# Transposed input for tiles 4 to 15, LayerNorm's factor applied behind the projections

## The chip, the cores and the metric

The kernel runs on one core of a Trainium2 chip. The metric is the device time of one execution in microseconds (us), shown as the median of several runs; the inputs are in the chip's memory before it starts. Engines are called by the names of the profile: PE (TensorE, matrix products), PEld (its weight loads), DVE (VectorE), ACT (ScalarE), POOL (GpSimd) and SP (SyncE, which issues all DMAs here).

## The reference

A block of 2048 tokens with 640 features: LayerNorm, attention with 32 heads of 20 features in a window of 256 tokens, a residual sum, and then a gated MLP that mixes tokens. Only the first part bears on this change:

```python
def _layernorm(x, axis=-1, eps=1e-5):
    m = jnp.mean(x, axis=axis, keepdims=True)
    v = jnp.var(x, axis=axis, keepdims=True)
    return (x - m) / jnp.sqrt(v + eps)

def _A_ref(x, wqkv, wo):
    B, S, D = x.shape                       # 1, 2048, 640
    H = 32; Dh = D // H; W = 256
    qkv = (lambda x, *d: x.transpose(*d))((x @ wqkv).reshape(B, S, 3, H, Dh), 2, 0, 3, 1, 4)
    q, k, v = qkv[0], qkv[1], qkv[2]
    scores = jnp.einsum("bhqd,bhkd->bhqk", q, k) * (Dh ** -0.5)
    ...
x = A_x
h = x + _A_ref(_layernorm(x, axis=-1), A_wqkv, A_wo)
```

LayerNorm's factor 1/sqrt(v + eps) is one number per token, so it may be applied to x before the product with the weights, or to the rows or columns of the product.

## The kernel before

**Value stage.** The tokens are 16 tiles of 128. For a tile i, `load_x` brings 128 tokens x 640 features; `ln1` (through `layernorm`, lines 74 to 80) takes its statistics on DVE (L74 to L76), raises the variance to the power -1/2 on POOL (L77) and subtracts the mean and multiplies by the factor on DVE (L80). `turn1` makes five transposes of 128x128 on PE (L469) into two PSUM banks; ACT copies them to a rounded high part (L473) and DVE makes the low part, the difference (L474). High and low parts of four tiles together fill one of the four chunks `xn_hi[c]`, `xn_lo[c]`, features first. `vgemm` multiplies a tile with the value weights: two halves of 320 columns, five feature blocks, three products each (high-high L485, high-low L486, low-high L487), so 30 products a tile, and ACT writes each half to `v_sb` (L488). The value weights arrive in raw form in ten pieces and are split by `split_wv`: the high part on ACT (L560), the low part on DVE or POOL (L561). A first stretch of 14 products with `ident` (L567) fills the time until the data is there.

**Query and key stage.** `qk_item(m, c)` makes one item: 128 rows m of queries or keys for the 512 tokens of chunk c, 15 products with 512 columns (L525 to L527), in one of two PSUM tiles. `split_qk` cuts the sum into three bf16 parts: ACT copies the first (L539), DVE subtracts it (L541), ACT copies the second (L543), POOL subtracts it for the third (L544), and SP stores all three to `qk_d` (L547). The steps of an item's split are issued during the next item's first two feature blocks. There are 40 items: 24 run alone, 4 more as a lead-in, and 12 are woven into the maximum stage.

**Maximum stage.** `max_item` makes scores for 128 queries against up to 384 keys (L333) and DVE takes each row's maximum (L339, one pass and one short reading of the result). 64 of these run with the 12 last items between them, one feature block of an item behind each. Each `max_item` takes one of three PSUM banks in turn. After eight blocks of queries `max_rows` turns the maxima into rows (L345, L348, L349). `load_stack` (L299) brings the stored parts back into the stacked form that the scores need.

PE, DVE, ACT and SP run their instructions in the order in which the code issues them; only POOL's order is left to the scheduler. So an instruction that waits holds up all behind it on its engine. The order at the start is written by hand:

```python
ln1(1, lambda: [split_wv(k, d, nc.vector) for k in (2, 4)])
for i in range(NT):
    if i + 3 < NT:
        load_x(i + 3)
    if i == 0:
        vgemm(0)
        ln1(2, lambda: turn1(1))
    elif i + 2 < NT:
        ln1(i + 2)
    if i == 1:
        vgemm(1)
    if 0 < i and i + 1 < NT:
        turn1(i + 1)
```

Of the kernel before, what the change touches and what calls it, by code (L numbers as in the profile page):

```python
# [34 lines left out]
def block_kernel(ctx, tc, x, wqk, wv, wo, w_in, wsp, bsp, w_out, out):  # L35
# [15 lines left out]
    r_d = dram.tile([H, S], F32, name="r_d")  # L51
    h_d = dram.tile([NT, P, D], F32, name="h_d")
# [175 lines left out]
    with ExitStack() as ab:  # L228
# [220 lines left out]
        if True:  # L449
# [3 lines left out]
            def load_x(i):  # L453
                xts[i] = tmp.tile([P, D], F32, tag="ta", bufs=3, name=f"xt{i}")
# [3 lines left out]
            def ln1(i, between=None):  # L458
                xn = tmp.tile([P, D], F32, tag="tb", bufs=2, name=f"xn{i}")
                layernorm(xn, xts.pop(i), D, f"a{i}", between)  # L460
# [15 lines left out]
            def vgemm(i):  # L476
                c, o = divmod(i, 4)
                t0 = o * P
                for j in range(2):
                    ps = s1_tile() if j else pv_tile(f"v{i}_{j}")  # L480
                    n0 = j * HD
                    for k in range(KD):
# [6 lines left out]
                                         ps[:, :HD].rearrange("p (h c) -> p h c", c=DH), AF.Copy)  # L489
# [3 lines left out]
            def load_wqk(m):  # L493
                raws[m] = tmp.tile([P, KD, P], F32, tag="wraw", bufs=5, name=f"wqraw{m}")
# [10 lines left out]
            def load_wo(k):  # L505
                raws[k] = tmp.tile([P, D], F32, tag="wraw", bufs=5, name=f"woraw{k}")
# [10 lines left out]
            def store_wo(k):  # L517
                for a, t in enumerate(wqs.pop(k)):
                    nc.sync.dma_start(wo_d[k, a], t.bitcast(F32))

# [15 lines left out]
            def split_qk(m, c, ps):  # L536
                sg = tmp.tile([P, 3, 512], BF16, tag="ta", bufs=3, name=f"sg{m}_{c}")
                rest = tmp.tile([P, 512], F32, tag="tb", bufs=2, name=f"rest{m}_{c}")
                nc.scalar.activation(sg[:, 0, :], ps, AF.Copy)  # L539
                yield  # L540
                nc.vector.tensor_tensor(out=rest, in0=ps, in1=sg[:, 0, :], op=OP.subtract)  # L541
                yield
                nc.scalar.activation(sg[:, 1, :], rest, AF.Copy)  # L543
# [8 lines left out]
            wv_raw = [tmp.tile([P, D], F32, tag="wraw", bufs=5, name=f"wvraw{k}") for k in range(KD)]  # L552
            for j, c in enumerate(halves):
                for k in range(KD):
                    nc.sync.dma_start(wv_raw[k][:, c], wv[k * P:(k + 1) * P, c])
                load_x(j + 1)
# [11 lines left out]
            ln1(0)  # L568
# [755 lines left out]
```

## Time and profile before

| what | us |
|---|---|
| median of 3 runs (lowest, highest) | 1129.86 (1129.74, 1132.98) |
| the profiled execution, its own time | 1132.73 |
| its span, first to last instruction | 1130.9 |
| PE busy in the span | 1093.7 |
| DVE busy in the span | 732.2 |
| ACT busy in the span | 565.9 |
| POOL busy in the span | 296.6 |
| value stage: first product of tile 0 to first query product | 8.86 to 91.86 |
| first maximum's scores to the last woven item's last product | 188.8 to 241.94 |

The profile is of one execution. A row of its timeline gives the start in us from the span's start, the duration in us, engine, line, operation, output and inputs, shapes, and in brackets the idle time of the engine just before and what ended it. PE's records overlap: a product's duration is longer than the distance to the next start, and the distance is what it takes of PE. A row of its busy times by stretches gives the stretch, its length, the busy us of the engines with the number of instructions, the clock that PE was granted (1.00 is full), the busy share of the DMA engines and the GB/s moved.

### The profile page before, as it was taken

Reading aid. Unit: us, or ns where it says so; the run is one execution under the profiler, and the core shown is the slowest. Engines: PE = TensorE matmul, PEld = TensorE weight load, DVE = VectorE, ACT = ScalarE, POOL = GpSimd, SP = SyncE. Lnnn points to the kernel's source line nnn. Section 1 sums busy time; section 2 is a strip of 40 time slices with the busy share of each in tenths; the row PEclk is TensorE's granted clock in tenths of the full one; section 3 lists DMA queues with packets and bytes.
Section 4 is the critical chain, followed back from the end, with each engine's and each line's share of the span. In section 5 each row is a group of like instructions: output and inputs, shape, how many; then the busy total and the mean of one; then the engine's idle time right before and its main releaser. Section 6 shows DMA issues by size and latency. Waiting matters only on the chain.

```text
span 1130.9 us, 28689 instructions
## 1 busy us (share of the span) xinstructions
PE 1093.7 (97%) x11180; PEld 986.3 (87%) x11180; DVE 732.2 (65%) x2060; ACT 565.9 (50%) x1169; POOL 296.6 (26%) x429
## 2 busy tenths in 40 slices
PE   8999999999999999889899999999999899999998
PEld 7998887667887777689799999999999799999998
DVE  6541123789999998478877678645458974656442
ACT  3433443249998989635566567433247521222210
POOL 3314444446666666612200011000001000000000
PEclk9999999999999999999999999999999999999999
DMA  5621346555565555489754522233251564444321
GB/s 183 224 72 68 136 141 239 176 178 170 184 188 175 181 170 158 143 241 305 255 185 165 181 90 76 85 122 101 100 162 57 176 193 135 123 148 138 103 87 61
DMA packets 83320, 171.78 MB, mean 152 GB/s; under 512 B 10944, under 2 KB 45248, under 8 KB 79296
## 3 DMA queue, kind: packets, MB, share of 16 engines
q1 hardware_dynamic: 83184, 169.95, 46.9%
q8 instruction: 88, 1.44, 0.6%
q14 instruction: 48, 0.39, 0.1%
HBM read 112.04 MB, written 57.87 MB: 150 GB/s over the span
## 4 chain that ended last, share of the span: by engine, by line
PE 74%; DVE 7%; DMA 7%; ACT 7%; issue 3%; POOL 1%; SPq 1%; DVEq 0%; ACTq 0%; POOLq 0%
PE g L1064 22%; PE out_ps L1129 8%; PE pv L425 5%; ACT pt L400 4%; PE zb L956 4%; PE qk L525 4%; PE qk L526 4%; PE qk L527 4%; PE bank L329 3%; PE bank L397 3%; PE zx L904 2%; PE zv L904 2%; DMA m<-o_d 2%; DMA wraw<-w_in_in 2%; PE zy L904 1%
## 5 line engine op out<-in xcount | busy, mean ns | idle before, releaser
L400 ACT ACTIVATE pt<-bank 128x384 f32<-128x384 f32 (+1 forms) x452 | 180.7, 477 | 19.9 <-PE bank L397 15.2
L721 ACT ACTIVATE aw<-fx 128x512 fp32r<-128x512 f32 (+2 forms) x160 | 93.5, 594 | 167.3 <-PE g L1064 122.6
L1064 PE MATMUL g<-zl,aw 128*128 128x432 f32 x768 | 171.8, 359 | 0.8 <-ACT zl L721 0.6
L339 DVE CUSTOM_DVE_ANT_0 junk<-bank,strip 128x288 bf16<-128x288 f32 x392 | 156.4, 454 | 14.0 <-PE bank L329 13.0
L1064 PEld LDWEIGHTS g<-zl,aw 128*128 128x128 f32 x768 | 143.7, 188 | 7.6 <-ACT zl L721 0.9
L425 PE MATMUL pv<-pt,v_sb 128*32 128x192 f32 (+3 forms) x1984 | 130.6, 322 | 7.5 <-ACT ot L441 3.5
L1064 PE MATMUL g<-ze,aw 128*128 128x432 f32 x576 | 134.8, 362 | 0.8 <-ACT aw L721 0.4
L715 DVE TENSOR_TENSOR aw<-fx,aw 128x512 fp32r<-128x512 f32 (+2 forms) x160 | 102.6, 646 | 37.9 <-ACT aw L721 36.7
L1064 PEld LDWEIGHTS g<-ze,aw 128*128 128x128 f32 x576 | 107.7, 189 | 7.0 <-ACT aw L721 1.6
L404 POOL TENSOR_SCALAR_AFFINE_SELECT pt<-pt 128x512 f32<-128x512 f32 x128 | 82.3, 644 | 61.9 <-ACT pt L400 58.2
L397 PE MATMUL bank<-slot 123*32 123x288 bf16 (+6 forms) x1296 | 94.0, 275 | 3.1 <-issue 2.2
L1129 PE MATMUL out_ps<-wout,y_sp 128*128 128x320 f32 (+1 forms) x630 | 96.2, 309 | 0.4 <-ACT y_sp L136 0.4
L956 PE MATMUL zb<-win,aw 128*128 128x432 f32 x480 | 95.3, 359 | 0.0
L1129 PEld LDWEIGHTS out_ps<-wout,y_sp 128*128 128x128 f32 (+1 forms) x630 | 94.1, 188 | 1.2 <-ACT y_sp L136 0.7
L329 PE MATMUL bank<-slot 120*32 120x288 bf16 (+6 forms) x1280 | 92.8, 277 | 1.9 <-DVE mcol L339 1.5
L956 PEld LDWEIGHTS zb<-win,aw 128*128 128x128 f32 x480 | 89.9, 187 | 5.0 <-ACT row L721 0.3
L86 POOL TENSOR_TENSOR mvz<-mvz,half 128x1 f32<-128x1 f32 x16 | 10.1, 633 | 303.3 <-DVE mvz L85 303.3
L541 DVE TENSOR_TENSOR rest<-qk,sg 128x512 f32<-128x512 f32 x40 | 27.7, 692 | 84.2 <-ACT sg L539 84.2
L425 PEld LDWEIGHTS pv<-pt,v_sb 128*32 128x32 f32 x1984 | 60.4, 110 | 18.7 <-issue 9.2
L715 DVE TENSOR_TENSOR row<-g,row 128x432 f32<-128x432 f32 x80 | 48.2, 604 | 37.6 <-PE g L1064 36.8
L407 POOL TENSOR_SCALAR_AFFINE_SELECT pt<-pt 128x512 f32<-128x512 f32 x112 | 72.5, 648 | 0.0
L397 PEld LDWEIGHTS <-slot 123*32 123x32 bf16 x1728 | 59.4, 97 | 14.1 <-issue 5.3
(185 smaller groups left out, 2233.0 us busy)
## 6 DMA issues: line engine op xcount, KB each, us to landing
slot<-qk_d SPq DMA_DIRECT2D x144, 160.0 KB
fx<-wsp_in SPq DMA_DIRECT2D x32, 512.0 KB
qk_d<-sg SPq DMA_DIRECT2D x40, 384.0 KB
fx<-hn_d SPq DMA_DIRECT2D x32, 320.0 KB
o_d<-ot SPq DMA_DIRECT2D x64, 128.0 KB
xb<-qk_d SPq DMA_DIRECT2D x48, 160.0 KB
z_d<-row SPq DMA_DIRECT2D x16, 432.0 KB
g_d<-row SPq DMA_DIRECT2D x16, 432.0 KB
```

The lines of the kernel that those rows point to most:

```text
L329: nc.tensor.matmul(ps[32 * j:32 * j + 32, o:o + w], one(st, 120, 0, hh, q0, 32), k, start=True, stop=True, tile_position=(0, 32 * j))
L339: nc.vector.tensor_tensor_reduce(out=junk[:, :n], in0=ps[:, :n], in1=keep, scale=1.0, scalar=NEG, op0=OP.add, op1=OP.max, accum_out=m_cols ...
L397: nc.tensor.matmul(ps[32 * i:32 * i + 32, b + o:b + o + w], one(st, 123, 1, hh, k0, 32), q, start=True, stop=True, tile_position=(0, 32 * i))
L400: nc.scalar.activation(pt[:, hh, :n], ps[:, :n], AF.Exp, scale=SCALE)
L404: nc.gpsimd.affine_select(out=pt[:, :, :P], in_=pt[:, :, :P], pattern=[[0, 4], [1, P]], base=0, channel_multiplier=-1, compare_op=OP.is_ge ...
L407: nc.gpsimd.affine_select(out=pt[:, :, 256:], in_=pt[:, :, 256:], pattern=[[0, 4], [-1, P]], base=-1, channel_multiplier=1, compare_op=OP. ...
L425: nc.tensor.matmul(ps[32 * hh:32 * hh + 32, a - 512 * c:b - 512 * c], v_sb[:, kb, v0:v0 + 32], pt[:, hh, a - kb * P:b - kb * P], start=fir ...
L715: (eng or nc.vector).tensor_tensor(out=out, in0=a, in1=b, op=op)
L721: nc.scalar.activation(out, a, AF.Copy)
L956: nc.tensor.matmul(b[0][:, :HF], a[t][:, x, kk], win2[0][:, y, kk, h * HF:(h + 1) * HF], start=kk + x + y == 0, stop=kk == KD - 1 and x == 1)
L1064: nc.tensor.matmul(ps, w[m][:, x, k], zc[k][m][:, y], start=start and k + x + y == 0, stop=stop and k == 3 and x == 1, skip_group_check=True)
L1129: nc.tensor.matmul(ps[j][:, :HD], src[:w, a, k, :], e1["wout"][:w, b, k, j * HD:(j + 1) * HD], start=(k == 0 and a + b == 0), stop=(k == K ...
```

## The change

The host lays x out a second time with the features first (`xt`). Tiles 0 to 3 keep their transposes on PE. For tiles 4 to 15 the transposed form is loaded (`load_xt`), and since the mean of a token is then needed along a row, `mean_row` makes it with one f32 product a tile: the column of means, spread over 128 columns, times `ident`, gives the means in every row. `turn1` subtracts that on DVE and makes high and low part from SBUF.

LayerNorm's factor is no longer applied to x. `stats1` leaves it in a column of `inv_std`. For the values it becomes the scale of ACT's copy to `v_sb`. For queries and keys it has to be a row over tokens: `store_std` transposes `inv_std`, stores it to `rstd_d`, and `load_std` loads the row of a chunk into all partitions. `split_qk` now begins with a multiplication by that row on DVE, which frees the PSUM tile, and the three parts are cut from the result in SBUF. So that one row serves two items, the 24 items run in pairs of m for each chunk. Buffers change with it: `ta` from 3 to 2, `tb` from 2 to 3, `wraw` from 5 to 3.

```diff
+            def stats1(i):
+                src = xts[i]
...
+                for j in range(2):
+                    nc.vector.bn_stats(out=st[:, j, :], in_=src[:, halves[j]])
+                nc.vector.bn_aggr(out=mv[:, 0:2], in_=st)
+                nc.vector.tensor_scalar(out=mv[:, 2:3], in0=mv[:, 1:2], scalar1=EPS, scalar2=None, op0=OP.add)
+                nc.gpsimd.tensor_tensor(out=inv_std[:, i:i + 1], in0=mv[:, 2:3], in1=half, op=OP.pow)
+
+            def center1(i):
+                xn = tmp.tile([P, D], F32, tag="tb", bufs=3, name=f"xn{i}")
+                nc.vector.tensor_scalar(out=xn, in0=xts.pop(i), scalar1=mvs.pop(i)[:, 0:1], scalar2=None,
+                                        op0=OP.subtract)
                 xns[i] = xn
+
+            def mean_row(i):
+                del xts[i]
+                rows1[i] = s2_tile()[:, :P]
+                nc.tensor.matmul(rows1[i], mvs.pop(i)[:, 0:1].to_broadcast([P, P]), ident, start=True, stop=True)
...
             def turn1(i):
                 xn = xns.pop(i)
                 c, o = divmod(i, 4)
+                if i >= TURNED:
+                    hi, lo = (v[c][:, :, o * P:(o + 1) * P] for v in (xn_hi, xn_lo))
+                    nc.vector.tensor_tensor(out=xn, in0=xn, in1=rows1.pop(i)[:, None, :].to_broadcast([P, KD, P]),
+                                            op=OP.subtract)
+                    nc.scalar.activation(hi, xn, AF.Copy)
+                    nc.vector.tensor_tensor(out=lo, in0=xn, in1=hi.bitcast(F32), op=OP.subtract)
+                    return
...
                     nc.scalar.activation(v4[:, i, 16 * j:16 * j + 16, :DH],
-                                         ps[:, :HD].rearrange("p (h c) -> p h c", c=DH), AF.Copy)
+                                         ps[:, :HD].rearrange("p (h c) -> p h c", c=DH), AF.Copy,
+                                         scale=inv_std[:, i:i + 1])
...
             def split_qk(m, c, ps):
-                sg = tmp.tile([P, 3, 512], BF16, tag="ta", bufs=3, name=f"sg{m}_{c}")
-                rest = tmp.tile([P, 512], F32, tag="tb", bufs=2, name=f"rest{m}_{c}")
-                nc.scalar.activation(sg[:, 0, :], ps, AF.Copy)
+                sg = tmp.tile([P, 3, 512], BF16, tag="ta", bufs=2, name=f"sg{m}_{c}")
+                rest = tmp.tile([P, 512], F32, tag="tb", bufs=3, name=f"rest{m}_{c}")
+                nc.vector.tensor_tensor(out=rest, in0=ps, in1=stds[c], op=OP.mult)
                 yield
-                nc.vector.tensor_tensor(out=rest, in0=ps, in1=sg[:, 0, :], op=OP.subtract)
+                nc.scalar.activation(sg[:, 0, :], rest, AF.Copy)
                 yield
+                nc.vector.tensor_tensor(out=rest, in0=rest, in1=sg[:, 0, :], op=OP.subtract)
                 nc.scalar.activation(sg[:, 1, :], rest, AF.Copy)
...
-            ln1(1, lambda: [split_wv(k, d, nc.vector) for k in (2, 4)])
+            stats1(1)
+            center1(1)
+            load_x(3)
+            for k in (2, 4):
+                split_wv(k, d, nc.vector)
             for i in range(NT):
-                if i + 3 < NT:
-                    load_x(i + 3)
                 if i == 0:
                     vgemm(0)
-                    ln1(2, lambda: turn1(1))
-                elif i + 2 < NT:
-                    ln1(i + 2)
-                if i == 1:
-                    vgemm(1)
-                if 0 < i and i + 1 < NT:
-                    turn1(i + 1)
+                    turn1(1)
+                    for n in (2, 3):
+                        stats1(n)
+                        center1(n)
+                        if n == 2:
+                            load_x(4)
+                else:
+                    if i + 3 < NT:
+                        load_xt(i + 3)
+                    if i + 4 < NT:
+                        load_x(i + 4)
+                    if i + 1 < NT:
+                        turn1(i + 1)
+                if TURNED <= i + 3 < NT:
+                    stats1(i + 3)
+                if TURNED <= i + 2 < NT:
+                    mean_row(i + 2)
...
-                if i > 1:
+                if i:
                     vgemm(i)
```

How the rows stand on PE at the start, before (`bank` and `v` are PSUM tiles, `xn_195` is tile 1, `xn_243` tile 2, `xn_263` tile 3, `slot` the value weights):

```order
L487 MATMUL bank_117<-slot_0_98,xa 128x320
L469 MATMUL bank_118<-ident,xn_195 128x128 x4
L469 MATMUL bank_119<-ident,xn_195 128x128
L485 MATMUL v_0_272<-slot_0_98,xa 128x320
...
L487 MATMUL bank_116<-slot_0_98,xa 128x320
L469 MATMUL bank_120<-ident,xn_243 128x128 x4
L469 MATMUL bank_118<-ident,xn_243 128x128
L469 MATMUL bank_119<-ident,xn_263 128x128 x4
L469 MATMUL bank_120<-ident,xn_263 128x128
```

And now (`xn_204` is tile 1, `xn_261` tile 2, `xn_272` tile 3, `mva_288` the statistics of tile 4):

```order
L528 MATMUL bank_118<-slot_0_99,xa 128x320
L510 MATMUL bank_119<-ident,xn_204 128x128 x4
L510 MATMUL bank_120<-ident,xn_204 128x128
L510 MATMUL bank_121<-ident,xn_261 128x128 x4
L510 MATMUL bank_119<-ident,xn_261 128x128
L526 MATMUL v_0_296<-slot_0_99,xa 128x320
...
L528 MATMUL bank_117<-slot_0_99,xa 128x320
L510 MATMUL bank_120<-ident,xn_272 128x128 x4
L510 MATMUL bank_121<-ident,xn_272 128x128
L485 MATMUL bank_119<-ident,mva_288 128x128
```

Tile 2's transposes have moved ahead of tile 1's products, and a mean row stands where two tiles' transposes followed each other. On DVE the same place read, from the end of tile 1's statistics to tile 2's normalising pass:

```order
L76 TENSOR_SCALAR mva_197<-mva_197 128x1
L561 TENSOR_TENSOR slot_1_99<-wvraw_129,slot_0_98 128x320
L561 TENSOR_TENSOR slot_1_99<-wvraw_131,slot_0_98 128x320
L80 TENSOR_SCALAR xn_195<-xt_137,mva_197 128x640
L74 BN_STATS sta_244<-xt_144 128x6 x2
L75 BN_AGGR mva_245<-sta_244 128x2
L76 TENSOR_SCALAR mva_245<-mva_245 128x1
L474 TENSOR_TENSOR xa<-bank_118,xa 128x4x128
L474 TENSOR_TENSOR xa<-bank_119,xa 128x128
L80 TENSOR_SCALAR xn_243<-xt_144,mva_245 128x640
```

And now:

```order
L473 TENSOR_SCALAR mva_198<-mva_198 128x1
L478 TENSOR_SCALAR xn_204<-xt_139,mva_198 128x640
L612 TENSOR_TENSOR slot_1_100<-wvraw_131,slot_0_99 128x320
L612 TENSOR_TENSOR slot_1_100<-wvraw_133,slot_0_99 128x320
L515 TENSOR_TENSOR xa<-bank_119,xa 128x4x128
L515 TENSOR_TENSOR xa<-bank_120,xa 128x128
L471 BN_STATS sta_254<-xt_170 128x6 x2
L472 BN_AGGR mva_255<-sta_254 128x2
L473 TENSOR_SCALAR mva_255<-mva_255 128x1
L478 TENSOR_SCALAR xn_261<-xt_170,mva_255 128x640
```

Tile 1 is centred (L478) ahead of the last two splits of the value weights, and tile 2's statistics stand behind tile 1's low part (L515) instead of ahead of it. In the maximum stage, DVE had between two items of a cycle (`junk` and `mcol` are a maximum and its reading, `rest` is an item's remainder, `qk` its PSUM tile):

```order
L339 ISA junk_2_2_1867,mcol_0_1788<-bank_115,mask 128x384
L339 ISA mcol_0_1788 128x1
L541 TENSOR_TENSOR rest_1_1870<-qk_1_1833,sg_1_1869 128x512
L339 ISA junk_2_3_1878,mcol_0_1788<-bank_117,mask 128x384
L339 ISA mcol_0_1788 128x1
```

And now:

```order
L587 TENSOR_TENSOR rest_1_1915<-qk_1_1878,std_1_1684 128x512
L340 ISA junk_4_0_1923,mcol_0_1792<-bank_116,mask 128x384
L340 ISA mcol_0_1792 128x1
L591 TENSOR_TENSOR rest_1_1915<-rest_1_1915,sg_1_1914 128x512
L340 ISA junk_4_1_1933,mcol_0_1792<-bank_118,mask 128x384
```

The multiplication (L587) stands one maximum ahead of the subtraction (L591), which needs ACT's copy of the product in between.

More of the change, by code (lines that the diff above doesn't have):

```diff
@@ L551, in block_kernel @@
             load_x(0)
-            wv_raw = [tmp.tile([P, D], F32, tag="wraw", bufs=5, name=f"wvraw{k}") for k in range(KD)]
+            wv_raw = [tmp.tile([P, D], F32, tag=("wraw", "wqh")[k > 2], bufs=(3, 4)[k > 2], name=f"wvraw{k}")
+                      for k in range(KD)]
             for j, c in enumerate(halves):
```

80 lines of the change are left out of this document (57 added, 23 removed).

## The prediction

> **What bounds the kernel now.** First the page: its first row says that TensorE is never far from busy, so a gain has to be a matmul that goes or a gap that closes. Then the busy time by stretches, since the change touches only the first 250 us.
>
> ```profile
> PE 1093.7 (97%) x11180; PEld 986.3 (87%) x11180; DVE 732.2 (65%) x2060; ACT 565.9 (50%) x1169; POOL 296.6 (26%) x429
> 30.00:40.00 10.00, 10.00 (x72) 9.99 (x71) 5.56 (x16) 4.64 (x11) 4.19 (x4) 1.00 0.65 229
> 200.00:220.00 20.00, 19.62 (x92) 12.34 (x90) 15.21 (x49) 4.91 (x8) 9.55 (x9) 1.00 0.54 174
> 220.00:240.00 20.00, 20.00 (x98) 12.80 (x97) 15.62 (x52) 6.06 (x10) 6.46 (x5) 1.00 0.60 196
> ```
>
> The columns after the stretch are its length and the busy us of PE, PEld, DVE, ACT and POOL, then clock, DMA share and GB/s. In the value stage (about 7 to 92 us) and where queries and keys are projected, PE has no gap and VectorE has room. In the maximum stage (189 to 242 us) PE is also full, but VectorE is at 15.2 to 15.6 of 20 us, and the change adds to it just there.
>
> **Saved on PE.** The timeline of PE around one value tile gives the price of its five transposes:
>
> ```profile
> 27.94 0.31 PE L487 MATMUL bank<-slot,xa 128*128 128x320 f32 x1
> 28.09 0.71 PE L469 MATMUL bank<-ident,xn 128*128 128x128 f32 x5
> 28.55 0.39 PE L485 MATMUL v<-slot,xa 128*128 128x320 f32 x1
> 28.78 0.31 PE L486 MATMUL v<-slot,xa 128*128 128x320 f32 x1
> 91.86 0.39 PE L525 MATMUL qk<-xa,wqh 128*128 128x512 f32 x1
> ```
>
> From the start of the transposes to the next product are 0.46 us, and that product takes 0.23 us to the next one where the others take 0.147: 0.085 more. A tile pays 0.545 us; 12 tiles pay 6.5 us. The check: from the start of tile 2's products (23.60, below) to 91.86 are 68.26 us, and 14 x 30 x 0.1467 + 12 x 0.545 = 68.2.
>
> **Added on PE.** Twelve mean rows and one transpose. No row shows a mean row in its place: it is f32, not a transpose, so two records. Nearest by place is the transpose, of the same shape and type at 0.46 / 5 = 0.09 us each: two make 0.18, 0.22 with some of the lead-in. The other end is the warm-up product, which is of the same kind:
>
> ```profile
> 1.77 5.96 PE L567 MATMUL bank<-ident 128*128 128x128 f32 x28 [1.77 <-POOL ident L59]
> ```
>
> 28 records for 14 products, 0.43 us each; with the lead-in 0.51. I take 0.22, since the warm-up stands at the program's start and the transposes stand where the mean rows will. The Trainium skill, "TensorE: Matmul & The Clock Gate", section "What's actually happening", says that the array starts at half its clock until it has been busy for about 3.4 us; by that the 0.43 would be 0.21 in a warm stage, while the page shows 1.00 there and so can't confirm it. 12 x 0.22 = 2.6, and 0.1 for the one transpose: **net -3.8 us**, between -6.5 + 2.2 + 0.1 = -4.2 and -6.5 + 6.1 + 0.1 = -0.3.
>
> The VectorE and ScalarE work per value tile stays about as it was (a normalising pass of 612 ns and two subtractions go, a subtraction of the mean and one low part come), within 5.6 of 10 us. Transfers grow by 320 KB a tile on a DMA share of 0.65 with 229 GB/s; each load is issued two tiles ahead, about 9 us, so I cost them at nothing. If that cover went, a late tile would stop PE for the lateness.
>
> **Lost at the start.** Here the order on PE and VectorE changes, and PE waits.
>
> ```profile
> 13.46 0.89 DVE L561 TENSOR_TENSOR slot<-wvraw,slot 128x320 fp32r<-128x320 f32 x2
> 14.01 0.41 PE L486 MATMUL bank<-slot,xa 128*128 128x320 f32 x1 [0.50 <-DVE slot L561]
> 14.40 0.61 DVE L80 TENSOR_SCALAR xn<-xt,mva 128x640 f32<-128x640 f32 x1
> 15.29 0.71 PE L469 MATMUL bank<-ident,xn 128*128 128x128 f32 x5
> 16.55 0.89 DVE L474 TENSOR_TENSOR xa<-bank,xa 128x512 fp32r<-128x512 f32 x2 [0.31 <-ACT xa L473]
> 17.36 0.60 DVE L80 TENSOR_SCALAR xn<-xt,mva 128x640 f32<-128x640 f32 x1
> 17.88 0.88 DVE L74 BATCH_NORM_STATS2 sta<-xt 128x6 f32<-128x320 f32 x2
> 19.03 0.15 DVE L76 TENSOR_SCALAR mva<-mva 128x1 f32<-128x1 f32 x1
> 23.60 0.39 PE L485 MATMUL v<-slot,xa 128*128 128x320 f32 x1
> ```
>
> Tile 1 is now centred before the two last splits of the value weights, which PE waits for at 14.01: 0.54 us later (14.40 to the next start at 14.93 in the row's own place). Tile 1's transposes move from 15.29 to 15.83, its low part from 16.55 to 17.09, ending after 0.81 at 17.90. Only then come tile 2's statistics, 1.23 us to the centring, and the centring of 0.61: 19.74. Tile 2's transposes now stand ahead of tile 1's products on PE, so **PE stands from about 16.4 to 19.8**; before, it ran tile 1's products there. They start at 19.80 + 0.47 = 20.27, tile 3's transposes at 20.27 + 4.48 = 24.75, tile 2's products at 25.22 without the mean row. Before it was 23.60: **+1.6 us**. I bound it by 1.0 (centring costs nothing at 14.01) and 2.5 (tile 2's load, issued behind tile 0's centring, lands after 17.90).
>
> **The clock.** That gap of 3.3 us may cost again. The stretches of 3.41 us that go with the two drops in the trace, and one without:
>
> ```profile
> 243.02:246.43 3.41, 1.63 (x34) 0.78 (x37) 3.37 (x18) 1.26 (x4) 2.55 (x3) 0.96 0.09 32
> 246.43:249.84 3.41, 3.41 (x64) 2.66 (x67) 2.86 (x14) 3.41 (x9) 2.43 (x6) 0.54 0.66 190
> 560.46:563.87 3.41, 1.34 (x8) 0.94 (x6) 0.47 (x1) 1.07 (x3) 0.72 (x2) 1.00 0.95 340
> 894.97:898.38 3.41, 1.24 (x7) 0.86 (x7) 3.41 (x7) 2.09 (x5) 0.00 (x0) 0.96 0.62 208
> ```
>
> After 1.63 and 1.24 us busy the clock went to about half for 3.41 us; after 1.34 it did not. A gap of 3.3 us leaves one such stretch with under 1.3 us busy in about two of three placements, and half speed for 3.41 us costs up to 1.7. I take **+1.3**, between 0 and 1.7; and the existing slow stretch at 246 may fall away in another placement, -1.7. The same page of the Trainium skill, section "HAM oscillation — how this bites in real kernels", warns only of PE gaps above about 3.4 us; by that this gap costs nothing and the sum is 1.3 lower, but the row at 243.02 shows a drop after a stretch that was never wholly idle.
>
> **Lost in the maximum stage.** Each of the 40 query and key items gets one more VectorE pass, from PSUM, and keeps its subtraction. Where PE has only these items, VectorE is mostly idle and the accumulator is free after one pass instead of two, so nothing is lost. In the maximum stage VectorE's cycle of five maxima is this:
>
> ```profile
> 198.11 0.69 DVE L541 TENSOR_TENSOR rest<-qk,sg 128x512 f32<-128x512 f32 x1
> 198.72 0.55 DVE L339 CUSTOM_DVE_ANT_0 junk<-bank,mask 128x384 bf16<-128x384 f32 x1
> 199.29 0.56 DVE L339 CUSTOM_DVE_ANT_0 junk<-bank,mask 128x384 bf16<-128x384 f32 x1
> 200.16 0.56 DVE L339 CUSTOM_DVE_ANT_0 junk<-bank,mask 128x384 bf16<-128x384 f32 x1 [0.30 <-PE bank L333]
> 202.47 0.69 DVE L541 TENSOR_TENSOR rest<-qk,sg 128x512 f32<-128x512 f32 x1
> 197.41 0.60 ACT L539 ACTIVATE sg<-qk 128x512 bf16<-128x512 f32 x1 [2.16 <-PE qk L527]
> 244.76 0.24 PE L329 MATMUL bank<-slot 120*32 120x128 bf16 x4 [1.26 <-DVE mcol L339]
> ```
>
> A cycle is 4.37 us of PE. VectorE uses 0.61 (198.11 to 198.72) + 5 x 0.57 = 3.46. Now 0.61 comes for the scaling, and the subtraction waits for ScalarE, which can start when the scaling ends: scaling at 0, copy at 0.72, subtraction 0.70 later (197.41 to 198.11) at 1.42, while the maximum between them ends at 1.18: 0.24 of waiting. 3.46 + 0.61 + 0.24 = 4.31 of 4.37: PE still decides, with three banks of slack, but VectorE can't catch up. The row of maxima halfway adds some 0.6 that stays: I take 0.35 of lateness at the end. There PE already waits 1.26 us for VectorE (244.76), so the last item's 0.61 + 0.24 and that lateness go straight on the path: **+1.2**, between 0.6 and 3.
>
> **Sum.** -3.8 + 1.6 + 1.3 + 1.2 = +0.3 us on the profiled execution's 1132.73 (span 1130.9 and 1.8 around it), so 1133.0 there. That execution lies 2.9 above the median of 1129.86, whose runs reach from 1129.74 to 1132.98; on the median the sum gives **1130.2**. A measurement of this kernel tells about 0.3%, 3.4 us, from no change.
>
> **Rivals.** *The gaps cost little*: the clock holds and the tail takes 0.6: -3.8 + 1.6 + 0.6 = -1.6, 1128.3, and with the slow stretch at 246 gone 1126.6; a mean row of 0.18 and a start of 1.0 bring 1125.5. For it speaks the row at 560.46, against it the row at 243.02.
>
> *VectorE becomes the bound of the maximum stage* (slower). It decides when its cycle passes 4.37, which 0.06 us is enough for. The subtraction now reads only SBUF, as the splits of the value weights do:
>
> ```profile
> 5.70 0.48 DVE L561 TENSOR_TENSOR slot<-wvraw,slot 128x320 fp32r<-128x320 f32 x1
> 11.14 1.17 DVE L561 TENSOR_TENSOR slot<-wvraw,slot 128x320 fp32r<-128x320 f32 x1
> ```
>
> The same pass took 0.48 alone and 1.17 beside GpSimd's. Were each subtraction 0.5 longer, 12 cycles would lose 12 x (4.81 - 4.37) = 5.3, less one bank's slack of 0.9: 0.3 + 4.4 gives 1134.6. The two output buffers instead of three could do the same through a late copy. Against it: GpSimd's pass of the item before ends about 0.4 us before the scaling starts. The Trainium skill, "SBUF — State Buffer", section "SBUF: two separate sides", says that VectorE with two SBUF inputs and GpSimd reading SBUF exclude each other for a whole instruction; the two rows agree, and by it the loss hangs on that 0.4 us.
>
> *The change does not save PE time*: a mean row at 0.51 costs 12 x 0.29 = 3.5 more: 1133.7.
>
> **How the numbers follow.** Forecast 0.67, gaps cheap 0.17, VectorE-bound 0.11, mean row dear 0.05. Of the second a half, and a little of the first, is faster than 1126.5: faster 0.10. Slower than 1133.2 are the third, most of the fourth and a few hundredths of the first: 0.15. Same: 0.75. The range leaves out the far ends of the second and third: 1126.4 to 1133.9; the forecast's own is 1127.5 to 1132.
>
> **What would show it.** The first query item should start near 89.7 + 1.3 instead of 91.86; a gap of some 3.3 us on PE, ended by VectorE's centring, should stand near 16.5; a clock row of about 0.5 soon behind it; the mean rows should be two records within 0.2 us; VectorE at 18 of 20 us in the maximum stage with PE full; the wait at its end about 2.4 instead of 1.26. I am wrong if PE waits inside the maximum stage, if loads stop PE between 25 and 60 us, or if the gap at 16.5 is filled.

## The result, and the profile after

| | before | after |
|---|---|---|
| median of 19 runs each on one chip, us (the lowest) | 1132.51 (1128.9) | 1139.38 (1134.63) |
| ratio of after to before, 95% interval | | 1.0053 [1.0037, 1.007] |
| the profiled execution's own time | 1132.73 | 1139.72 |
| its span | 1130.9 | 1138.0 |

The change makes the kernel slower by half a per cent; on the 1129.86 of the prediction the ratio gives 1135.8, above the range. One of after's 19 runs took 2159.28 us, and the ratio leaves it out. The two profiles differ by 7.1 us of span and the medians by 6.9; a second profile of before (e15) is 1.9 us longer than the first, so the totals of two profiles alone prove little. The page's first row and the busy time by stretches, of the kernel after:

```profile
PE 1096.5 (96%) x11145; PEld 986.1 (87%) x11145; DVE 759.2 (67%) x2088; ACT 569.2 (50%) x1158; POOL 297.1 (26%) x429
```

```profile
30.00:40.00 10.00, 10.00 (x71) 10.00 (x70) 5.61 (x13) 4.63 (x8) 4.32 (x5) 1.00 0.70 221
200.00:220.00 20.00, 19.86 (x91) 12.46 (x89) 17.03 (x55) 5.65 (x9) 9.27 (x7) 1.00 0.53 176
220.00:240.00 20.00, 19.97 (x99) 12.77 (x99) 17.30 (x54) 5.72 (x10) 7.11 (x7) 1.00 0.63 205
17.74:21.15 3.41, 1.50 (x11) 1.50 (x12) 3.20 (x11) 0.77 (x2) 0.97 (x2) 0.96 0.13 23
21.15:24.56 3.41, 3.41 (x15) 3.41 (x14) 2.25 (x7) 0.52 (x1) 0.90 (x2) 0.54 0.95 305
```

The value stage is as full as before and loads don't stop it. VectorE in the maximum stage went from 15.2 and 15.6 to 17.0 and 17.3 of 20 us, with PE still full there. So the loss is not where the busy time grew most; it has to be looked for stage by stage. The timeline of after at the places that the prediction named:

```profile
14.48 0.41 PE L527 MATMUL bank<-slot,xa 128*128 128x320 f32 x1 [0.94 <-DVE slot L612]
19.65 0.77 PE L510 MATMUL bank<-ident,xn 128*128 128x128 f32 x5 [3.19 <-DVE xn L478]
20.17 0.39 PE L526 MATMUL v<-slot,xa 128*128 128x320 f32 x1
26.19 0.71 PE L510 MATMUL bank<-ident,xn 128*128 128x128 f32 x5
26.74 0.39 PE L485 MATMUL bank<-ident,mva 128*128 128x128 f32 x2
26.88 0.39 PE L526 MATMUL v<-slot,xa 128*128 128x320 f32 x1
91.13 0.39 PE L573 MATMUL qk<-xa,wqh 128*128 128x512 f32 x1
192.84 0.22 PE L334 MATMUL bank<-slot 120*128 120x128 bf16 x1 [0.77 <-DVE mcol L340]
195.98 0.27 PE L334 MATMUL bank<-slot 120*128 120x256 bf16 x1 [1.35 <-DVE mcol L340]
246.10 0.32 PE L334 MATMUL bank<-slot 120*128 120x384 bf16 x1 [0.33 <-DVE mcol L340]
247.37 0.24 PE L330 MATMUL bank<-slot 120*32 120x128 bf16 x4 [0.95 <-DVE mcol L340]
248.61 0.24 PE L330 MATMUL bank<-slot 120*32 120x128 bf16 x4 [0.88 <-DVE mcol L340]
250.61 0.43 PE L398 MATMUL bank<-slot 123*32 123x288 bf16 x4 [0.78 <-ACT pt L401]
```

The gap at the start, the clock's half-speed stretch behind it (0.54) and the two-record mean row are there as forecast. New are two waits of PE inside the maximum stage, at 192.84 and 195.98. At the stage's end PE waits 0.33, 0.95 and 0.88 us for VectorE and 0.78 for ScalarE, 2.9 in sum; before it waited there 0.33 (at 243.18) and 1.26 (244.76) for VectorE and 0.37 (246.34) for ScalarE, 2.0 in sum.

Cut at the same events in every profile, the span falls into six stages. Three kernels were profiled twice (before again as e15, e3 as e10, e7 as e11): their lone stages, maximum stages and junctions repeat to 0.1 us, but the start moves by up to 1.0, the score stage by up to 4.9 and the rest by up to 2.3. The table has all 17 profiled executions of this study:

```text
us          start  lone  maximum  junction  score  rest    span
before       91.9  97.0   52.5      8.0     222.3  659.2  1130.9
e15          90.9  97.0   52.5      8.0     222.9  661.5  1132.8
after        91.1  98.2   54.9      9.3     223.3  661.1  1138.0
e1           87.7  98.2   56.0      9.3     225.5  660.9  1137.7
e2           90.4  98.2   52.4      9.1     222.1  660.8  1133.0
e3           88.0  98.2   52.4      9.2     223.1  660.5  1131.4
e4           97.4  97.0   52.5      7.4     227.7  659.6  1141.7
e5           91.7  97.0   52.5      7.9     224.3  660.1  1133.6
e6           95.2  97.1   52.5      7.8     223.7  658.9  1135.3
e7           88.2  98.2   52.4      9.3     219.2  661.5  1128.7
e8           91.2  99.6   54.2      9.3     223.9  661.7  1139.9
e9           90.7 100.3   54.3      7.4     224.1  663.5  1140.2
e10          88.7  98.2   52.4      9.3     225.2  658.8  1132.6
e11          88.6  98.2   52.4      9.3     224.1  660.2  1132.8
e12          90.7  97.0   52.5      7.9     224.9  662.9  1135.9
e13          90.7  96.9   55.3      9.3     220.6  660.5  1133.2
e14          88.9  96.9   52.3      9.1     220.0  662.4  1129.5
```

*start*: to the first query product. *lone*: from there to the first maximum's scores (24 items alone on PE, then four with other work). *maximum*: to the last feature block of the last woven item (its L525 at 241.34 in before, L573 at 244.26 in after; the expectations below call this the item's last product). *junction*: to the first product of scores and values (L425 in before, L426 in after). *score*: to the last score product; the expectations count this stage from its first product instead, some 4 to 6 us earlier, and so find it longer (226.8 us in before). *rest*: to the end. Between before and after the stages give -0.7 (91.86 to 91.13), +1.2, +2.4, +1.3, +1.0 and +1.9: the 7.1 us.

### The profile page after: what moved, and what is told of

Its sections match the earlier page's. It is cut to its first block, busy times and chain, and to the rows that moved or that the text cites. A ratio compares the mean times of both kernels' runs of the same rounds, so it can differ in the third digit from the quotient of the medians.

```text
span 1138.0 us, 28707 instructions
## 1 busy us (share of the span) xinstructions
PE 1096.5 (96%) x11145; PEld 986.1 (87%) x11145; DVE 759.2 (67%) x2088; ACT 569.2 (50%) x1158; POOL 297.1 (26%) x429
## 4 chain that ended last, share of the span: by engine, by line
PE 72%; ACT 8%; DVE 8%; DMA 7%; issue 3%; POOL 1%; SPq 0%; ACTq 0%; DVEq 0%; POOLq 0%
PE g L1142 22%; PE out_ps L1207 8%; PE pv L426 5%; PE zb L1034 4%; ACT pt L401 4%; PE bank L330 3%; PE bank L398 3%; PE qk L573 3%; PE qk L575 3%; PE qk L574 3%; PE zx L982 2%; DMA qk_d<-sg 2%; PE zv L982 2%; DMA wraw<-w_in_in 2%; PE zy L982 1%
## 5 line engine op out<-in xcount | busy, mean ns | idle before, releaser
L426 PE MATMUL pv<-pt,v_sb 128*32 128x192 f32 (+3 forms) x1984 | 130.4, 324 | 8.5 <-ACT ot L442 3.7
L398 PE MATMUL bank<-slot 123*32 123x288 bf16 (+7 forms) x1296 | 94.0, 277 | 0.8 <-ACT pt L401 0.8
L426 PEld LDWEIGHTS pv<-pt,v_sb 128*32 128x32 f32 x1984 | 59.8, 110 | 20.4 <-issue 10.3
L593 POOL TENSOR_TENSOR sg<-rest,sg 128x512 bf16<-128x512 f32 x40 | 46.7, 1167 | 86.2 <-ACT sg L592 68.1
```

The costliest lines, as they stand in the source:

```text
L398: nc.tensor.matmul(ps[32 * i:32 * i + 32, b + o:b + o + w], one(st, 123, 1, hh, k0, 32), q, start=True, stop=True, tile_position=(0, 32 * i))
L426: nc.tensor.matmul(ps[32 * hh:32 * hh + 32, a - 512 * c:b - 512 * c], v_sb[:, kb, v0:v0 + 32], pt[:, hh, a - kb * P:b - kb * P], start=fir ...
```

## The experiments

Each edit is told against the kernel named; each ratio is to before on the same chip, with its 95% interval.

**The start.** e1 puts after's start back into before's order.

```diff
# e1_start: after, with
-    center1(1) ahead of split_wv(2), split_wv(4)
+    split_wv(2), split_wv(4) ahead of center1(1)
-    turn1(1); stats1(2); center1(2); ...; turn1(2); vgemm(1)
+    stats1(2); turn1(1); center1(2); ...; vgemm(1); turn1(2)
```

> The changed kernel with the order at its start as before the change: tile 1's products ahead of tile 2's transposes, the two value-weight splits ahead of tile 1's centring, tile 2's statistics ahead of tile 1's low part. Theory (the gap of 3.19 us and the half-speed stretch that follows it are on the path): no PE gap over 1 us between 15 and 24 us, clock 1.00 in 20 to 30 us, first query product at about 88.2 instead of 91.13 (1.6 from the order, 1.3 to 1.7 from the clock), time about 3 us below the changed kernel. Rival (the start is made up for later, by waits that end on loads): first query product earlier, but the last woven item ends at 244.3 as now and the time is the same.

First query product at 87.7, 3.4 us earlier; the gap of 3.19 us and the half-speed stretch at 21 are gone. The ratio is 1.0036 [1.0015, 1.0057] against after's 1.0053, a difference of about 1.9 us in the total, but the two intervals are too wide to tell 1.9 from 3.4 or from nothing. In the profiled execution 0.3 us reached the end, because the maximum stage took 1.1 and the score stage 2.2 more. The start's price is confirmed, its worth at the end is not.

**The ring of output buffers.** e2 gives the three pieces of an item (tag `ta`) three buffers again and `tb` two; e3 has both edits.

```diff
# e2_ring3: after, with
-    sg = tmp.tile([P, 3, 512], BF16, tag="ta", bufs=2, ...)
+    sg = tmp.tile([P, 3, 512], BF16, tag="ta", bufs=3, ...)
-    rest = tmp.tile([P, 512], F32, tag="tb", bufs=3, ...)
+    rest = tmp.tile([P, 512], F32, tag="tb", bufs=2, ...)
# (x and x transposed use the same tags; load_xt(i + 3) moves behind turn1(i + 1))
```

> The changed kernel with three output buffers for the three parts of an item instead of two (and two remainder buffers instead of three, each transposed tile loaded after the one before it has been used). Theory (late copies that wait for a store of two items ago hold VectorE, and through it the maxima): ScalarE's wait for stores falls from 18.4 us between 160 and 250 to under 3, PE's waits of 0.77 and 1.35 at the head of the maximum stage go, the last woven item's last product starts 2 to 2.5 us earlier than 244.3, time 2 to 3 us below the changed kernel. Rival (VectorE's added pass alone bounds the stage): these PE waits stay, and the last item ends within 0.5 us of 244.3.

> Both edits together. Theory: they add up, first query product near 88.2 and the last woven item at about 239, ahead of the kernel before (241.3); time 5 to 6 us below the changed kernel, within 2 us of the kernel before, on either side, since clock drops later on may fall differently. Rival (one of the two covers the other): no more than 3 us below the changed kernel.

The maximum stage is 52.4 us in e2 and e3: all of its 2.4 us comes back, while the lone stage stays as in after and the junction within 0.2 us of it. The waits between 160 and 250 us say by what. In before, where no store appears among ScalarE's waits:

```profile
DVE rest L541 <- ACT sg L539: 22.8, 10, 2.8
PE bank L333 <- DVE mcol L339: 0.3, 1, 0.3
```

In after:

```profile
DVE rest L591 <- ACT sg L589: 25.1, 22, 3.8
ACT sg L589 <- DMA qk_d<-sg: 18.4, 10, 3.6
PE bank L334 <- DVE mcol L340: 2.4, 3, 1.3
```

and in e2 of the same three lines only two are left:

```profile
DVE rest L591 <- ACT sg L589: 8.9, 21, 0.7
PE bank L334 <- DVE mcol L340: 0.3, 1, 0.3
```

A row names the waiting engine and line, what it waited for, the sum in us, the times and the longest. In after ScalarE's first copy waits ten times for a store to leave its buffer, up to 3.6 us; VectorE's subtraction waits for that copy; the maxima stand behind the subtraction in VectorE's order; PE waits for the maxima. With a third buffer the store wait is gone from the view. The chain at the head of after's maximum stage, ahead of PE's two waits at 192.84 and 195.98:

```profile
191.22 0.63 ACT L589 ACTIVATE sg<-rest 128x512 bf16<-128x512 f32 x1 [1.75 <-DMA qk_d<-sg]
191.88 0.69 DVE L591 TENSOR_TENSOR rest<-rest,sg 128x512 f32<-128x512 f32 x1 [2.48 <-ACT sg L589]
194.36 0.63 ACT L589 ACTIVATE sg<-rest 128x512 bf16<-128x512 f32 x1 [1.12 <-DMA qk_d<-sg]
195.02 0.69 DVE L591 TENSOR_TENSOR rest<-rest,sg 128x512 f32<-128x512 f32 x1 [1.43 <-ACT sg L589]
```

These two waits of PE are 2.1 of the 2.4 us. After's twelve store waits from 91 us on run from 131.38 to 202.66: nine stand in the lone stage, where PE doesn't feel them, and three at the head of the maximum stage; behind 203 us no first copy waits for a store. Ratio of e2: 1.0019 [0.9998, 1.004]; of e3: 1.0005 [0.9989, 1.0021].

**Is it the ring alone, or the added pass?** e9 leaves the multiplication out, and with it the factor on queries and keys, but keeps two buffers.

```diff
# e9_nomult: after, with
-    nc.vector.tensor_tensor(out=rest, in0=ps, in1=stds[c], op=OP.mult)
-    yield
-    nc.scalar.activation(sg[:, 0, :], rest, AF.Copy)
+    nc.scalar.activation(sg[:, 0, :], ps, AF.Copy)
     yield
-    nc.vector.tensor_tensor(out=rest, in0=rest, in1=sg[:, 0, :], op=OP.subtract)
+    nc.vector.tensor_tensor(out=rest, in0=ps, in1=sg[:, 0, :], op=OP.subtract)
```

> Kernel after without the factor on queries and keys: the multiplication is left out and the first piece is copied from the product's bank as in before (so queries and keys lack the factor); the loads of the factor, two output buffers and the paces of the loads stay. If VectorE's added work is what costs the maximum stage 2.5 us, the time from its first maximum to the last woven product falls from 55.0 to 52.5 us as in before, and the junction to the score stage loses its 1.3 us too. If the ring of two buffers does it by itself, it stays at 54 to 55 us. And for the lone stage: 96.9 us from the first query product to the first maximum if the multiplication took the steps of 0.68 us away, 98.2 us if not.

The junction falls to 7.4 us, so its +1.3 is the added pass, which comes last on VectorE there. A part of this fall is the clock: after has 4.0 us at half speed inside the junction, e9 none, and e4, which has before's code there and no half speed either, takes 7.4 us too. Kernels alike in the clock, e2 and e6 with 2.1 us of half speed each, take 9.1 and 7.8 us, so the pass costs 1.3. The maximum stage stays at 54.3, so two buffers cost 1.8 of the 2.4 us without any added pass; the rest takes both. The store wait stands in the same view:

```profile
ACT sg L587 <- DMA qk_d<-sg: 16.1, 7, 3.8
PE bank L334 <- DVE mcol L340: 0.6, 2, 0.3
```

Here a late copy holds the accumulator itself, and PE's query products wait for that instead: "[0.98 <-DVE rest L589]" at 187.38, at the end of the lone stage (100.3 us), and "[1.23 <-DVE rest L589]" at 192.47, in the maximum stage. Ratio 1.0037 [1.0014, 1.006].

**The lone stage.** In it PE waits for nothing in before or in after, but the products go at another rate. Two stretches of equal length, before first:

```profile
91.80:188.80 97.00, 97.00 (x422) 78.75 (x420) 18.67 (x27) 39.53 (x66) 45.67 (x36) 1.00 0.45 155
```

```profile
91.80:188.80 97.00, 97.00 (x416) 77.97 (x415) 38.59 (x53) 38.47 (x63) 43.42 (x34) 1.00 0.58 178
```

Six products fewer in the same busy 97 us. In before three products take 0.68 us for part of each matrix's items (those that read the normalised tiles from `xb`) and 0.70 for the others; in after always 0.70 or 0.71. e8 restores the order of the items, e9 above leaves out the multiplication, e13 only pads a tile:

```diff
# e8_order: after, with the 24 lone items as
-    q, r = divmod(n, 8); m, c = 2 * q + r % 2, r // 2
+    m, c = divmod(n, 4)       # and load_std((n + 1) % 4) for each item
# e13_align: after, with
-    inv_std = tmp.tile([P, NT], F32, name="inv_std")
+    inv_std = tmp.tile([P, P], F32, name="inv_std")[:, :NT]
```

> Kernel after, with the 24 lone query/key items in the order of before (matrix outside, chunk inside) instead of two matrices a chunk, and so a load of the factor for each item. If the order of the items is why no step of three products takes 0.68 us any more, the stage from the first query product to the first maximum takes 96.9 us as in before, not 98.2, and the total falls by about 1.3. If it is the multiplication that reads the products, or where the chunks lie, it stays at 98.2.

> Kernel after with the tile of the factors (16 columns, 64 bytes a partition) padded to 512 bytes, so that every tile allocated behind it, the query/key weights among them, starts at a multiple of 512 bytes again as in before; nothing else changes. If the places of the weights are why no step of three products takes 0.68 us in after, the stage from the first query product to the first maximum falls from 98.2 to 96.9 us, and the total by 1 to 1.5 us. If not, 98.2 us.

In e8 and e9 every step still takes about 0.70 (the rest of their 99.6 and 100.3 us are waits; e8's ratio is 1.0065 [1.0039, 1.009]); in e13 the 0.68 is back in the items that read `xb`, the stage takes 96.9 us, and the products of the stretch are as many as in before:

```profile
90.60:187.60 97.00, 97.00 (x423) 78.81 (x421) 38.77 (x53) 39.01 (x64) 43.93 (x34) 1.00 0.57 178
```

The 64 bytes a partition of `inv_std` had moved every tile allocated behind it in its pool off multiples of 512 bytes. That this costs PE 1.3 us here is shown. By the addresses in the built programs the only moved operands of these products are the weights; `xb` starts at a multiple of 512 bytes in all three kernels and `xa` 224 bytes behind one, which fits the steps of 0.68 us standing only where weights and `xb` are both in place. The weights alone were not moved in a run. In the total 1.3 us can't be told from nothing: 1.0047 [1.0029, 1.0065] against 1.0053.

**Why the same delay doesn't cost the same at the end.** e4 adds TensorE work to before, ahead of the first query product.

```diff
# e4_shift24: before, with, ahead of the first query item
+    for n in range(24):
+        nc.tensor.matmul(fill[:, :P], ident, ident, start=True, stop=True)
```

> The kernel before the change with 24 more f32 products of ident with itself ahead of the first query product, nothing else; they cost 24 x 0.22 = 5.3 us and move all that follows by about as much as the change does. Theory (the clock is judged on a fixed grid of 3.41 us, so a pure shift decides whether later PE gaps, near 500 and 565 us, are followed by half speed): half-speed stretches appear near 505 and 570 as in the changed kernel, and the time is 7 to 9 us above the kernel before. Rival (those stretches come from the change itself): time 5.3 us above, no new half-speed stretch after 300 us.

The ratio is 1.0081 [1.0051, 1.0112]. 5.6 us came in at the first query product and 10.8 at the end: the score stage took 5.4 more with nothing changed in it. Half-speed stretches stand at 513 and 574 us, near where the theory put them; but e15 below has one near 501 without any shift, so this doesn't show that the shift made them. The waits and the timeline of e4 name no engine for that:

```profile
PE bank L397 <- issue: 6.9, 8, 1.6
```

```profile
298.35 0.28 PE L397 MATMUL bank<-slot 123*32 123x288 bf16 x1 [1.29 <-issue]
358.63 0.30 PE L397 MATMUL bank<-slot 123*32 123x288 bf16 x2 [1.59 <-issue]
```

"issue" means that nothing which the profile shows was waited for. PE's records, numbered as they start, show what it is. In the 17 executions PE pauses for over 0.3 us 103 times between 6 us into the stage and its last 20 us, and all 103 stand at one place of a block of 256 records, weight loads and waits included (59 behind the 194th of the count, 44 behind the 193rd), also the 18 that the profile puts down to an engine. The page's DMA part has a queue "instruction" with 88 packets, 1.44 MB in before: 16 KB each, and 88 times 256 is 22528, where PE has 22519 records. The last packet lands 1.1 to 1.7 us ahead of each of the 103 restarts, in e4 at 296.90, 307.58 and 357.19, with restarts at 298.35, 309.16 and 358.63; where PE passes the place without a pause, the packet has mostly landed earlier (2.1 us ahead in the median). In the score stage PE's small products use up such a block in about 4.5 us (50 of them in 227 us); the next packet mostly starts 0.5 to 2.6 us after a border and takes 0.9 to 2.2 us, and where it is late PE stops. The sums of these stalls over the whole stage: before 4.2 us, e15 3.7, after 4.4, e1 6.8, e4 9.5.

Does it matter where the borders fall? The next runs move them without other work: fewer or more, wider or narrower warm-up products.

```diff
# e5_code24: before;  e6_time24: before;  e7_both_w4: e3_both;  e12_before_w4: before
-    14 warm-up products of 128 columns
+    e5: 38 narrow ones (96 instructions more)
+    e6: 7 of 256 columns, and 7 wide ones ahead of the first query item (none more)
+    e7, e12: 3 of 512 columns and one of 256 (40 instructions fewer)
```

> Kernel before, with its 14 warm-up products of 128 columns replaced by 38 narrow ones (2 weight columns, 48 moving columns): 96 more TensorE instructions ahead of everything, as in e4_shift24, but no added time. Theory (code blocks: TensorE's instructions are loaded in blocks of 256, 16 KB each, and in the score stage a block lasts about as long as the loading of the next, so where the block borders fall sets the stalls): first query product within 1 us of 91.9, but the score stage 230 to 233 us long instead of 226.9, with stalls of about 8 to 10 us in sum that end at every 256th instruction, as in e4; total 3 to 6 us over before. Rival (the moment at which the stage starts, by the clock's grid or by what else runs, sets its length): score stage 226 to 228 us and the total within 1 us of before.

> Kernel before, with the same added TensorE time as e4_shift24 ahead of the first query product (7 wide products of 3072 columns in sum) but 7 fewer, wider products in the warm-up, so that the count of instructions ahead of every later one is that of before. Theory (code blocks): first query product near 97.3 as in e4, score stage 226 to 228 us long with stalls at block borders of about 4 us in sum as in before; total 5 to 7 us over before, 3 to 5 under e4. Rival (the moment sets the length): score stage 231 to 232 us as in e4, total 8 to 11 over before.

> e3_both (start order of before, ring of three output buffers) with the warm-up as 4 wide products in place of 14: 40 fewer TensorE instructions ahead of everything, so every block border falls 40 instructions later in the program. Theory (code blocks): the score stage's length changes by up to 3 us with no change in it; with the borders moved so that the short blocks are less often complete ones, 226 to 228 us instead of 229.1, total 1 to 3 us under e3_both, so 1130.5 to 1132.5, ratio to before about 0.998. Rival: 229 us and a ratio of 1.000, as in e3.

> e3_both once more, to stand on one chip beside e11. Score stage 228 to 230 us, ratio to before 0.999 to 1.002.

> e7_both_w4 once more, beside e10 on one chip: the two differ in the number of warm-up products alone. Theory (code blocks): score stage 225 to 226 us, stalls at block borders under 3 us in sum, and 2 to 3 us less than e10 in the median. Rival (the shorter stage is given back to the clock or to later waits): the medians agree within 1 us.

> Kernel before with the warm-up of e7, 40 fewer TensorE instructions ahead of everything: block borders move in before as they did from e10 to e11. Theory (code blocks): stalls at other instructions than in before, with a sum of 1 to 6 us instead of 4.2 and a score stage that differs from 226.9 us by the same; nothing else moves. Rival (block borders have no part in it): score stage 226.5 to 227.5 us with the stalls where they were.

The answer is mixed. By the expectations' count the score stage is 226.8 and 227.4 us in the two profiles of before, 228.7 in e5, 228.1 in e6, 225.3 in e7, 231.3 in e10, 230.2 in e11 and 229.3 in e12; e5, e7, e10 and e11 are outside what was expected of them. Both ways of moving the borders in before made it slower, e5 by 1.0035 [1.0016, 1.0054] with 6.0 us of stalls, e12 by 1.0036 [1.0018, 1.0054] with 5.3, though their first four stages are those of before. e6, with its borders where before has them, has 5.4 us of stalls, which decides nothing, since one kernel had 1.6 and 4.1 in two executions (e7 and e11); its 3.3 us of added time (less than the 5.3 meant) became 1.0053 [1.0034, 1.0072]. e7 had the shortest span of all and a ratio of 1.0002 [0.9982, 1.0022], but e11, the same kernel, stands beside e10 with medians of 1132.79 and 1134.11 us and ratios of 1.0015 [0.9994, 1.0037] and 1.0017 [0.9996, 1.0037]. That the stalls are late code blocks is shown; that a place of the borders can be chosen that avoids them is not.

**How much belongs to a single execution, and is there a faster version?** e15 profiles before again; e14 has e3's two edits, e7's warm-up and e13's padding.

> Kernel before, unchanged, profiled a second time. If the score stage's length and the half-speed stretches belong to the single execution and not to the program (theory: stalls at the same place in the code block but not always at the same blocks; the clock's grid starts at another moment in every execution), the score stage is 225 to 231 us with stalls at block borders of 2 to 6 us and a half-speed stretch near 500 or 566 us may appear; the first query product, first maximum and last woven product stay within 0.5 us of 91.9, 188.8 and 241.3. If they belong to the program: 226.9 us and the stalls at 344, 378 and 410 us again.

> Start order of before, ring of three output buffers, wide warm-up (e7) and the padded tile of e13 together. If e13's theory holds: first maximum near 185.0 us, last woven product near 237.5, and a median 2 to 4 us under before, ratio 0.996 to 0.999. If not: as e7 and e11, ratio 1.000 to 1.002.

e15 has its lone, maximum and junction stages within 0.1 us of the first profile, its first query product 1.0 earlier, four stalls of which two stand at blocks that stalled in the first profile too and two elsewhere, and half-speed stretches at 467 and 501 that the first did not have. So the score stage and the rest belong in part to the single execution. e14 has each repaired stage where it should be, 96.9 and 52.3 us, and a ratio of 0.9987 [0.9969, 1.0004]: with every loss but the junction's repaired, what the change saves can't be told from nothing.

## Why the prediction was wrong, step by step

**Saved on PE: right.** The mean row takes its two records and 0.22 us with the lead-in, as forecast; a turned tile's period is 4.62 us where it was 4.95. With before's start in its place (e1) the first query product comes 4.15 us earlier than in before; forecast was 3.8.

**Lost at the start, and the clock: right in mechanism.** The gap ran from 16.46 to 19.65 (forecast 16.4 to 19.8) and was ended by the centring; the clock row is 0.54. Tile 1's products start at 20.17 (forecast 20.27) and take 6.02 us to 26.19 instead of 4.48, so the clock cost 1.5 (forecast 1.3). The first query product came 0.7 us earlier, forecast 0.9; e15 shows that this moment moves by 1.0 us between executions, so its nearness is in part luck.

**"Where PE has only these items ... nothing is lost": failed, +1.2 us.** PE waits for nothing there, as I said, but its steps got longer, because a small new tile moved the ones behind it (e13). A stage without waits was taken for a stage without cost.

**"Lost in the maximum stage, +1.2, between 0.6 and 3": the main failure, it was +3.8.** The step that failed is "PE still decides": the sum priced VectorE's added work and put the step from three output buffers to two at nothing. The work itself was priced well. With three buffers the stage is as long as before (52.4 us in e2 and e3 against 52.5), behind 203 us of after the subtraction waits 0.28 us an item for ScalarE (forecast 0.24), and the end costs +1.3 in the junction (forecast 0.85 + 0.35 = 1.2). The sign named for being wrong, PE waiting inside the stage, came true at 192.84 and 195.98. The missing term is the 2.4 us there. It stood in the rival as half a sentence: two output buffers, through a late copy. It should have been in the sum. The change takes the ring from 3 to 2, and puts loads of the factor and bunches of three slot loads into the queue that carries the stores (48 slot loads between 160 and 250 us in both, but 5 loads of 256 KB more). A store's way through that queue was never compared with the time between items, which is shortest in the lone stage, where the lateness built up. The runs show the ring's part; what the loads' order adds was not tried by itself.

**The rivals.** The mean row was not dear. VectorE did not become the bound: the time, 1135.8, came out near that rival's 1134.6, but by the buffers, not by a longer subtraction, which takes 0.69 us in the median in before and in after. Of the two rows shown for a longer pass, the one read as alone (0.48 us at 5.70) was not: a pass of GpSimd starts at 5.78. The gaps did not cost little.

**Behind 250 us I had no term.** The profiles differ there by 1.0 and 1.9 us; the table shows a spread of 219 to 228 and of 659 to 663 us in stages that the edits don't touch, with late code blocks and half-speed stretches among the causes. The first four stages account for 4.3 of the measured 6.9 us; how much of the rest is the change's own doing stays open. e5 and e12 are some 4 us slower than before with no loss in the first four stages, so 2.6 us can arise without a further loss of the change; that they do is not shown. The repair agrees: e14 has 6.5 us less than after in the first four stages, and by the ratios 0.66% or 7.5 us less, to some 3 us.

## What to carry to other kernels

When a change takes a buffer from a ring, put the ring into the sum: the longest time from a buffer's first write to the landing of its store, with all that is queued ahead of that store, against the ring's length times the shortest time between items. Compare stages cut at the same events, and take a second profile of the same kernel ahead of believing any of them; what repeats to 0.1 us is the program's, the rest may be the execution's. Let a new small tile fill the unit that its neighbours are aligned to.

## What the runs showed of the hardware

**The clock has a grid.** In every execution the half-speed stretches start at whole multiples of 3.41333 us, to 0.002 us, from the first moment of full clock, which itself lay anywhere from 4.66 to 7.77 us of the span. Three windows of after on that grid, each followed by a stretch at half speed:

```profile
246.14:249.55 3.41, 1.47 (x30) 0.58 (x30) 3.14 (x13) 1.26 (x2) 2.00 (x2) 1.00 0.35 120
502.14:505.55 3.41, 0.63 (x5) 0.36 (x3) 1.73 (x4) 1.03 (x2) 0.00 (x0) 1.00 0.99 368
566.99:570.40 3.41, 0.28 (x1) 0.28 (x2) 1.34 (x3) 1.94 (x4) 0.00 (x0) 1.00 0.92 358
```

Over the 17 executions, windows at full clock with under 1.2 us of PE busy were followed by a drop 18 times of 18, those with 1.2 to 1.6 us 37 of 41, with 1.6 to 1.8 us 5 of 12, with 1.8 to 2.4 us 4 of 89, and fuller ones never in 5357. So a gap of 2.8 us can cost a drop or none, by where the grid cuts it: in before the gap near 499 us lay across a border (2.22 and 1.84 us busy) and cost nothing, in e15 most of it fell into one window (1.38 us busy) and half speed followed. The stretches in which the prediction read 1.63, 1.24 and 1.34 us lie 0.3 us behind this grid; on it they hold 1.67 and 1.46 (half speed followed) and 1.64 (it didn't), so the bound is nearer to 1.6 us than to the 1.3 that it took. The Trainium skill, "TensorE: Matmul & The Clock Gate", section "What's actually happening", has the window of 3413 ns and says that it runs freely, without regard to the kernel's start; the executions agree. Its rule, in the section "HAM oscillation — how this bites in real kernels", that there should be no PE-idle gaps above about 3.4 us is too kind: none of the three windows above was wholly idle.

**Code arrives in blocks**, 16 KB for 256 TensorE instructions, through the DMA engines, and a stage of products under 0.1 us each can outrun it. **Tiles moved by 64 bytes** off multiples of 512 cost TensorE 1.3 us in 97, with no wait in any view; other distances were not tried.
